# Retention attention and SwiGLU: y computed turned in 32-column TensorE tiles, scores over all rows, the own-token term on A's diagonal, the MLP one step earlier

## The chip, the cores and the metric

The kernel runs on one core of one Trainium2 chip. The metric is device time in microseconds (us). TensorE, VectorE, ScalarE and GpSimd appear in the profile as PE (PEld for its weight loads), DVE, ACT and POOL.

## The reference

Sizes are B=4, H=8, S=768, D=48 for the attention, and 3072 tokens, 384 model columns and 1536 hidden columns for the feed-forward block. Everything is fp32.

```python
for t in range(S):
    kt, vt, rt = k[:, :, t], v[:, :, t], r[:, :, t]
    cur = einsum('bhd,bhe->bhde', u * kt, vt)              # the token's own term
    y[:, :, t] = einsum('bhd,bhde->bhe', rt, state + cur)
    state = w * state + einsum('bhd,bhe->bhde', kt, vt)
x = y.transpose(0, 2, 1, 3).reshape(B * S, H * D)
g = x @ w_gate
out = (g * sigmoid(g) * (x @ w_val)) @ w_out
```

## The kernel before

The sequence is cut into 24 chunks of 128 tokens (6 in time x 4 batches), and the attention runs in chunked form. A head pair shares 128 partitions: 48 rows, 16 empty rows, 48 rows, 16 empty rows. The program is a pipeline of steps. In step s it prepares chunk s+1, turns chunk s, makes the scores of chunk s-1 and the outputs of chunk s-2, and turns x of chunk s-3. Between these parts it feeds *pieces* of the feed-forward block (MLP): a piece is six matmuls of `gv` or four of `o_ps`. Before the MLP can run, its 18 weight blocks are rounded by ACT, VectorE and GpSimd.

```python
def prepare(i):                       # GpSimd, then VectorE
    pool.tensor_mul(khat[i % 4][:], kl[:], kscale[:])
    pool.tensor_mul(rhat[i % 2][:], rl[:], rscale[:])
    pool.tensor_mul(rk[:], rl[:, :, 0:D], kl[:, :, 0:D])
    pool.tensor_mul(rk[:], rk[:], ub[:])
    dve.tensor_reduce(du[:], rk[:], axis=AX.X, op=ALU.add)
    ...
def scores(i, e):                     # e: which head of each pair
    q = slice(64 * e, 64 * e + D)     # 48 of the 128 rows
    for a in range(HP):
        pe.matmul(ps[:, a, :], kT[q, a, :], rT[q, a, :], start=True, stop=True, ...)
    dve.copy_predicated(At[i % 2][:, e], mask..., ps[:])
def own(i):                           # dv = du * v, on VectorE, two multiplies
    ...
def outputs(i):
    for a in range(HP):               # 128 tokens x 96 columns of y
        if c > 0:
            pe.matmul(ps[:, a, :], rT[:, a, :], Z[b][:, a, :], start=True, stop=False, ...)
        for e in range(2):
            pe.matmul(ps[:, a, :], A[:, e, a, :], vl[:, a, e, :], ...)
    dve.tensor_add(xs[i][:], ps..., dvs.pop(i)...)
def turn_x(i):                        # three transposes, then ACT
    for c in range(CC):
        pe.transpose(tp[:, c, :], x[:, P * c : P * (c + 1)], ident[:])
    act.copy(xT[:, i % NX, :, :], tp[:])
# ... the loop over steps (cut)
for s in range(N + 3):
    per = [0] * 6 if s < 4 else [1, 0, 1, 0, 1, 0] if s < 8 else [1] * 6 if s < 10 else [2] * 6
```

Of the kernel before, what the change touches and what calls it, by code (L numbers as in the profile page):

```python
# [9 lines left out]
FP32 = mybir.dt.float32  # L10
INT32 = mybir.dt.int32
# [4 lines left out]
P = 128  # L16
# [6 lines left out]
def fast(  # L23
# [24 lines left out]
    nc = tc.nc  # L48
    B, H, S, D = r.shape
    DP = 64  # L50
    HP = H // 2
    NCH = S // P
    N = B * NCH
    DM, DFF = moe_w_gate.shape
    CC, FC = DM // P, DFF // P

    cst = ctx.enter_context(tc.tile_pool(name="cst", bufs=1))
    two = ctx.enter_context(tc.tile_pool(name="two", bufs=2))
    three = ctx.enter_context(tc.tile_pool(name="three", bufs=3))
    ps_a = ctx.enter_context(tc.tile_pool(name="ps_a", bufs=5, space=bass.MemoryType.PSUM))  # L60
    ps_f = ctx.enter_context(tc.tile_pool(name="ps_f", bufs=2, space=bass.MemoryType.PSUM))
    ps_o = ctx.enter_context(tc.tile_pool(name="ps_o", bufs=1, space=bass.MemoryType.PSUM))
    dve, pool, act, pe, sp = nc.vector, nc.gpsimd, nc.scalar, nc.tensor, nc.sync


    wcol = cst.tile([P, HP], FP32, name="wcol")
    ub = cst.tile([P, H, D], FP32, name="ub")
    kscale = cst.tile([P, H, DP], FP32, name="kscale")
    rscale = cst.tile([P, H, DP], FP32, name="rscale")
    wL = cst.tile([P, HP, 2 * D], FP32, name="wL")  # L70
    sq = cst.tile([P, 8, HP], FP32, name="sq")
    bad = cst.tile([P, HP], FP32, name="bad")
    held = cst.tile([P, HP], FP32, name="held")
    badc = cst.tile([P, 1], FP32, name="badc")
    ones = cst.tile([P, 1], FP32, name="ones")
    ident = cst.tile([P, P], FP32, name="ident")
    mask = cst.tile([P, P], FP32, name="mask")
# [3 lines left out]
    NX = 12  # L81
    xT = cst.tile([P, NX, CC, P], FP32, name="xT")
    Z = [cst.tile([P, HP, 2 * D], FP32, name=f"Z{b}") for b in range(B)]
    r_ld = [cst.tile([P, H, DP], FP32, name=f"r_ld{i}") for i in range(2)]
    k_ld = [cst.tile([P, H, DP], FP32, name=f"k_ld{i}") for i in range(2)]

    v_ld = [cst.tile([P, HP, 2, 2 * D], FP32, name=f"v_ld{i}") for i in range(4)]
    khat = [cst.tile([P, H, DP], FP32, name=f"khat{i}") for i in range(4)]
    rhat = [cst.tile([P, H, DP], FP32, name=f"rhat{i}") for i in range(2)]
    At = [cst.tile([P, 2, HP, P], FP32, name=f"At{i}") for i in range(2)]  # L90

    def v_heads(i):
        t = v_ld[i % 4]
        return [t[:, :, e, D * e : D * (e + 1)] for e in range(2)]

    def load(i):
        c, b = divmod(i, B)
# [4 lines left out]
    def load_v(i):  # L102
        c, b = divmod(i, B)
        rows = slice(P * c, P * (c + 1))
        for e, dst in enumerate(v_heads(i)):
            sp.dma_start(
                out=dst, in_=v[b, :, rows, :].rearrange("(a e) t d -> e t a d", e=2)[e]
            )


# [51 lines left out]
    for t in k_ld + r_ld:  # L162
        dve.memset(t[:, :, D:DP], 0.0)
    for t in v_ld:
        dve.memset(t[:], 0.0)
    for e in range(2):
        sp.dma_start(out=wcol[64 * e : 64 * e + D, :], in_=w.rearrange("(a e) d -> e d a", e=2)[e])
    load(0)
# [1 line left out]
        out=ub[:].rearrange("p h d -> p (h d)"),  # L170
        in_=bass.AP(tensor=u.tensor, offset=u.offset, ap=[[0, P], [1, H * D]]),
# [14 lines left out]
    for l in range(7):  # L186
        n = 1 << l
        f = sq[:, l, :].unsqueeze(2).to_broadcast([P, HP, n])
# [8 lines left out]
    for e in range(2):  # L197
        q = slice(64 * e, 64 * e + 64)
# [6 lines left out]
        out=mask[:], in_=mask[:], compare_op=ALU.is_gt, fill=0.0,  # L205
        base=0, pattern=[[1, P]], channel_multiplier=-1,
    )
    for t in At:
        pool.memset(t[:], 0.0)


    dve.tensor_tensor(bad[:], held[:], wcol[:], ALU.not_equal)
# [4 lines left out]
    act.copy(outside, n_ps[0:1, 0, 0:1])  # L217


    dus, dvs, xs, turned = {}, {}, {}, {}  # L220

    def prepare(i):
        kl, rl = k_ld[i % 2], r_ld[i % 2]
# [9 lines left out]
        if i + 2 < N:  # L233
            load(i + 2)

    def turn(i):
        got = []
        for nm, t in (("kT", khat[i % 4]), ("rT", rhat[i % 2])):
            tp = ps_a.tile([P, HP, P], FP32, name="tp", tag="a")
            for a in range(HP):  # L240
                pe.transpose(  # L241
                    tp[:, a, :], t[:, 2 * a : 2 * a + 2, :].rearrange("p e d -> p (e d)"), ident[:]
                )
            x = (two if nm == "kT" else three).tile([P, HP, P], FP32, name=nm, tag=nm)
            act.copy(x[:], tp[:])
            got.append(x)
        turned[i] = got

    def scores(i, e):
        kT, rT = turned[i]  # L250
        q = slice(64 * e, 64 * e + D)
        ps = ps_a.tile([P, HP, P], FP32, name="s_ps", tag="a")
        for a in range(HP):
            pe.matmul(  # L254
                ps[:, a, :], kT[q, a, :], rT[q, a, :],
                start=True, stop=True, skip_group_check=True,
            )
        dve.copy_predicated(  # L258
            At[i % 2][:, e], mask[:].bitcast(INT32).unsqueeze(1).to_broadcast([P, HP, P]), ps[:]
        )  # L260

    def own(i):
        du = dus.pop(i)
        dvs[i] = two.tile([P, HP, 2, D], FP32, name="dv", tag="dv")
        for e, vh in enumerate(v_heads(i)):
            dve.tensor_mul(
                dvs[i][:, :, e, :], vh,
                du[:].rearrange("p (a e) -> p a e", e=2)[:, :, e : e + 1].to_broadcast([P, HP, D]),
            )

    def outputs(i):
        c, b = divmod(i, B)
        A, vl = At[i % 2], v_ld[i % 4]
        rT = turned.pop(i)[1]
        ps = ps_a.tile([P, HP, 2 * D], FP32, name="y_ps", tag="a")
        for a in range(HP):
            if c > 0:
                pe.matmul(  # L278
                    ps[:, a, :], rT[:, a, :], Z[b][:, a, :],
                    start=True, stop=False, skip_group_check=True,  # L280
                )
            for e in range(2):
                pe.matmul(  # L283
                    ps[:, a, :], A[:, e, a, :], vl[:, a, e, :],
                    start=(c == 0 and e == 0), stop=(e == 1), skip_group_check=True,
                )
        xs[i] = two.tile([P, DM], FP32, name="xs", tag="xs")
        dve.tensor_add(  # L288
            xs[i][:], ps[:].rearrange("p a x -> p (a x)"),
            dvs.pop(i)[:].rearrange("p a e d -> p (a e d)"),  # L290
        )

    def update(i):
        c, b = divmod(i, B)
        if c == NCH - 1:
            return
        kh, vl, z = khat[i % 4], v_ld[i % 4], Z[b]
        ps = ps_a.tile([P, HP, 2 * D], FP32, name="u_ps", tag="a")
        for a in range(HP):
            pe.matmul(  # L300
                ps[:, a, :].rearrange("p (e d) -> p e d", e=2),
                kh[:, 2 * a : 2 * a + 2, :].rearrange("p e d -> p (e d)"),
                bass.AP(
                    tensor=vl.tensor, offset=vl[:, a, 0, :].offset,
                    ap=[list(vl[:].ap[0]), [3 * D, 2], [1, D]],
                ),
                start=True, stop=True, skip_group_check=True,
            )
        if c == 0:
            dve.tensor_mul(z[:], ps[:], wL[:])  # L310
        else:
            dve.tensor_add(z[:], ps[:], z[:])  # L312
            pool.tensor_mul(z[:], z[:], wL[:])  # L313

    def turn_x(i):
        tp = ps_a.tile([P, CC, P], FP32, name="xtp", tag="a")
        x = xs.pop(i)
        for c in range(CC):
            pe.transpose(tp[:, c, :], x[:, P * c : P * (c + 1)], ident[:])  # L319
        act.copy(xT[:, i % NX, :, :], tp[:])  # L320


    hT = {}
# [41 lines left out]
    def feed(n):  # L365
        for _ in range(min(n, len(todo))):
            todo.popleft()()

    def queue(g):
        for f in range(FC):  # L370
            todo.append(lambda g=g, f=f: gate_value(g, f))
            if g > 0 and f >= 2 and f < 8:
                todo.append(lambda g=g, n=f - 2: project(g - 1, n // 3, n % 3))

    prepare(0)
    for s in range(N + 3):

        per = [0] * 6 if s < 4 else [1, 0, 1, 0, 1, 0] if s < 8 else [1] * 6 if s < 10 else [2] * 6
        if s + 1 < N:
            prepare(s + 1)  # L380
        if s < N:
            turn(s)
        round_weights(1 if s else 0)
        feed(per[0])
        if 1 <= s <= N:
            scores(s - 1, 0)
            feed(per[1])
            scores(s - 1, 1)
            own(s - 1)
            feed(per[2])  # L390
        if s >= 3:
            turn_x(s - 3)
            if s % 2 == 0:
                queue((s - 4) // 2)
            feed(per[3])
        if 2 <= s <= N + 1:
            outputs(s - 2)
            feed(per[4])
            update(s - 2)
        round_weights(1 if s > 1 else 0)  # L400
        feed(per[5])
    feed(len(todo))
    for j in range(2):
        for part in range(3):
# [414 lines left out]
```

## Time and profile before

The first line of the table is device time; the others are of one profiled execution.

| | before |
|---|---|
| time, median of 4 runs | 795.25 us (795.05 to 795.78) |
| span of the profiled run, mean granted clock | 793.2 us, 0.975 |
| turn of chunk 8, of chunk 10 | 122.7 us, 174.7 us |
| a full step after chunk 10 | 38.4 us |
| last matmul | 787.2 us |

"Turn of chunk i" is the first transpose of chunk i's keys on the TensorE timeline. I use it as a clock for the pipeline. From its first 175 us one should keep two things: the work is handed back and forth between GpSimd and VectorE, and TensorE has gaps.

### The profile page before, as it was taken

How to read it: one execution, taken by the hardware profiler on the slowest of the kernel's cores; microseconds unless marked ns; L12 is line 12 of the kernel's file. 1: busy time of each engine (PE TensorE's matmuls, PEld its weight loads, DVE VectorE, ACT ScalarE, POOL GpSimd, SP SyncE). 2: the span in 40 equal slices, each digit the busy share in tenths (PEclk: the TensorE clock that was granted, in tenths of full speed). 3: DMA queues.
4: the chain of work that ended last, by engine and by line, in shares of the span. 5: the costliest groups of instructions: out<-in, count | busy, mean ns of one | idle time of the engine just before them, and what ended most of it. 6: DMA issues, size and time to landing. Idle time of an engine off the chain costs nothing.

```text
span 793.2 us, 8984 instructions
## 1 busy us (share of the span) xinstructions
PE 749.0 (94%) x3666; PEld 604.1 (76%) x3666; DVE 250.3 (32%) x520; ACT 137.0 (17%) x281; POOL 159.0 (20%) x142
## 2 busy tenths in 40 slices
PE   3878888999999999999999999999999999999996
PEld 2777776877878878878878778778878878878773
DVE  5554565633222323222223223223223123212120
ACT  2432222411111111111111111111111111011010
POOL 5756454360202020202020202202202000000000
PEclk9958898999999999999999999999999999999999
DMA  8755454111101020102010102101000000000000
GB/s 206 149 154 134 119 151 113 50 41 31 30 11 41 1 40 11 31 11 41 0 41 11 31 10 41 31 11 41 10 11 22 1 11 10 1 11 11 10 11 23
DMA packets 85761, 33.89 MB, mean 43 GB/s; under 512 B 76368, under 2 KB 79568, under 8 KB 85712
## 3 DMA queue, kind: packets, MB, share of 16 engines
q1 hardware_dynamic: 82256, 28.52, 15.8%
q10 hardware_dynamic: 3456, 4.72, 1.7%
q8 instruction: 31, 0.51, 0.3%
q14 instruction: 18, 0.15, 0.1%
HBM read 28.51 MB, written 4.72 MB: 42 GB/s over the span
## 4 chain that ended last, share of the span: by engine, by line
PE 81%; DVE 8%; POOL 8%; issue 2%; ACT 1%; DMA 0%; SPq 0%; POOLq 0%; DVEq 0%
PE gv L333 45%; PE o_ps L352 22%; PE s_ps L254 4%; PE y_ps L283 4%; PE y_ps L278 2%; POOL khat L225 2%; POOL rhat L226 2%; PE tp L241 2%; DVE wo L156 1%; PE u_ps L300 1%; POOL rk L228 1%; POOL rk L227 1%; POOL wg L157 1%; PE xtp L319 1%; DVE wg L156 1%
## 5 line engine op out<-in xcount | busy, mean ns | idle before, releaser
L333 PE MATMUL gv<-xT,wg 128*128 128x256 f32 x864 | 217.6, 388 | 13.8 <-DVE hT L341 11.5
L333 PE MATMUL gv<-xT,wv 128*128 128x256 f32 x864 | 214.5, 385 | 0.0
L352 PE MATMUL o_ps<-wo,hT 128*128 128x384 f32 x576 | 197.1, 486 | 0.6 <-ACT o_sb L358 0.6
L333 PEld LDWEIGHTS gv<-xT,wg 128*128 128x128 f32 x864 | 158.1, 192 | 38.8 <-issue 11.5
L333 PEld LDWEIGHTS gv<-xT,wv 128*128 128x128 f32 x864 | 167.3, 194 | 23.8
L340 DVE TENSOR_TENSOR sg<-sg,gv 128x256 f32<-128x256 f32 x144 | 60.5, 420 | 326.6 <-ACT sg L339 326.6
L352 PEld LDWEIGHTS o_ps<-wo,hT 128*128 128x128 f32 x576 | 109.0, 190 | 62.9 <-ACT o_sb L358 1.2
L339 ACT ACTIVATE sg<-gv 128x256 f32<-128x256 f32 x144 | 55.2, 383 | 493.0 <-PE gv L333 480.7
L313 POOL TENSOR_TENSOR Z<-Z,wL 128x384 f32<-128x384 f32 x16 | 16.4, 1027 | 394.9 <-DVE Z L312 394.9
L283 PE MATMUL y_ps<-v_ld,At 128*128 128x96 f32 x384 | 61.7, 293 | 0.7 <-issue 0.7
L341 DVE TENSOR_TENSOR hT<-sg,gv 128x256 f32<-128x256 f32 x144 | 60.5, 420 | 4.9
L254 PEld LDWEIGHTS s_ps<-rT,kT 48*128 48x128 f32 x384 | 46.9, 210 | 18.1 <-issue 14.8
L254 PE MATMUL s_ps<-rT,kT 48*128 48x128 f32 x384 | 54.4, 310 | 2.2 <-DVE At L258 2.2
L283 PEld LDWEIGHTS y_ps<-v_ld,At 128*128 128x128 f32 x384 | 54.7, 209 | 1.0 <-issue 0.9
L258 DVE COPY_PREDICATED At<-mask,s_ps 128x512 f32<-128x512 int32 x48 | 33.5, 726 | 42.5 <-PE s_ps L254 42.3
L230 DVE TENSOR_REDUCE du<-rk 128x8 f32<-128x384 f32 x24 | 13.2, 552 | 83.1 <-POOL rk L228 83.1
L225 POOL TENSOR_TENSOR khat<-k_ld,kscale 128x512 f32<-128x512 f32 x24 | 30.5, 1272 | 6.2 <-ACT kscale L195 6.2
L226 POOL TENSOR_TENSOR rhat<-r_ld,rscale 128x512 f32<-128x512 f32 x24 | 30.5, 1272 | 2.1 <-ACT outside L217 2.1
L278 PE MATMUL y_ps<-Z,rT 128*128 128x96 f32 x160 | 30.4, 271 | 0.0
L278 PEld LDWEIGHTS y_ps<-Z,rT 128*128 128x128 f32 x160 | 25.7, 192 | 3.1
L288 DVE TENSOR_TENSOR xs<-y_ps,dv 128x384 f32<-128x384 f32 x24 | 13.3, 555 | 46.3 <-PE y_ps L283 46.3
L300 PEld LDWEIGHTS u_ps<-v_ld,khat 128*128 128x128 f32 x160 | 23.2, 211 | 2.7
(63 smaller groups left out, 356.5 us busy)
## 6 DMA issues: line engine op xcount, KB each, us to landing
k_ld<-in_k_dram SPq DMA_DIRECT2D x24, 192.0 KB, 3.2
r_ld<-in_r_dram SPq DMA_DIRECT2D x24, 192.0 KB, 3.6
w_bits<-in_moe_w_gate_dram SPq DMA_DIRECT2D x6, 768.0 KB, 5.0
w_bits<-in_moe_w_val_dram SPq DMA_DIRECT2D x6, 768.0 KB, 4.7
v_ld<-in_v_dram SPq DMA_DIRECT2D x48, 96.0 KB, 3.1
w_bits<-in_moe_w_out_dram SPq DMA_DIRECT2D x6, 768.0 KB, 4.5
out_dram<-o_sb ACTq DMA_DIRECT2D x24, 192.0 KB, 1.9
ub<-in_u_dram SPq DMA_DIRECT2D x1, 192.0 KB, 5.0
```

What stands on the lines that cost most here:

```text
L225: pool.tensor_mul(khat[i % 4][:], kl[:], kscale[:])
L226: pool.tensor_mul(rhat[i % 2][:], rl[:], rscale[:])
L254: pe.matmul(ps[:, a, :], kT[q, a, :], rT[q, a, :], start=True, stop=True, skip_group_check=True,)
L258: dve.copy_predicated(At[i % 2][:, e], mask[:].bitcast(INT32).unsqueeze(1).to_broadcast([P, HP, P]), ps[:])
L278: pe.matmul(ps[:, a, :], rT[:, a, :], Z[b][:, a, :], start=True, stop=False, skip_group_check=True,)
L283: pe.matmul(ps[:, a, :], A[:, e, a, :], vl[:, a, e, :], start=(c == 0 and e == 0), stop=(e == 1), skip_group_check=True,)
L300: pe.matmul(ps[:, a, :].rearrange("p (e d) -> p e d", e=2), kh[:, 2 * a : 2 * a + 2, :].rearrange("p e d -> p (e d)"), bass.AP(tensor=vl.t ...
L333: pe.matmul(gv[:, o, :].rearrange("p (i t) -> p i t", i=2), wt[:, c, P * f : P * (f + 1)], xT[:, 2 * g % NX : 2 * g % NX + 2, c, :], start ...
L339: act.activation(sg[:], gv[:, 0, :], AF.Sigmoid)
L340: dve.tensor_mul(sg[:], sg[:], gv[:, 0, :])
L341: dve.tensor_mul(hT[g][:, f, :], sg[:], gv[:, 1, :])
L352: pe.matmul(ps[:], hT[g][:, f, P * j : P * (j + 1)], wo[:, f, :], start=(f == 0), stop=(f == FC - 1),)
```

## The change

Its intent is to spend less TensorE time on attention. The scores use all 128 rows, with zeros where the other head of a pair sits. The own-token term is written on the diagonal of A by GpSimd, so no separate `dv` and no add are needed. And y is computed already turned: v and the state are the weights, in blocks of 32 columns, one block for each 32 of y_ps's 128 partitions (called column tiles below; `128*32` in the profile), so turning x falls away. The pipeline is one step shorter and the MLP is queued one step earlier.

```diff
+    def diagonal(i):
+        pool.tensor_mul(
+            At[i % 2][:], ident[:].unsqueeze(1).to_broadcast([P, H, P]),
+            dus.pop(i)[:].unsqueeze(2).to_broadcast([P, H, P]),
+        )
 def turn(i): ...
+            if nm == "kT":
+                for e in range(2):
+                    q = slice(64 * e, 64 * e + 64)
+                    act.copy(kT[i % 2][q, :, e, :], tp[q])
 def scores(i, half): ...
-                ps[:, a, :], kT[q, a, :], rT[q, a, :],
+                ps[:, n, :], kT[i % 2][:, a, e, :], turned[i][:, a, :],
 def outputs(i): ...
+        for cc in range(CC):
+            rows = []
+            for q in range(4):
+                a, s = divmod(4 * cc + q, 3)
+                each = [(z[:, a, 32 * s : 32 * s + 32], rT[:, a, :])] if c > 0 else []
+                if s < 2:
+                    each.append((vl[:, a, 32 * s : 32 * s + 32], A[:, 2 * a, :]))
+                if s > 0:
+                    each.append((vl[:, a, 32 * s + 16 : 32 * s + 48], A[:, 2 * a + 1, :]))
+                rows.append(each)
+            for n in range(3):
+                for q in range(4):
+                    if n < len(rows[q]):
+                        pe.matmul(ps[32 * q : 32 * q + 32, cc, :], *rows[q][n], ...)
+        act.copy(xT[:, i % NX, :, :], ps[:])
-    def own(i): ...      # and turn_x
 # ... (cut: v_ld's layout, clearing of kT instead of At and v_ld)
-        per = [0] * 6 if s < 4 else [1, 0, 1, 0, 1, 0] if s < 8 else [1] * 6 if s < 10 else [2] * 6
+        per = [0] * 5 if s < 3 else [1, 0, 1, 0, 1] if s < 8 else [1] * 5 if s < 10 else [3, 2, 2, 3, 2]
+        if 1 <= s <= N:
+            diagonal(s - 1)
         if s + 1 < N:
             prepare(s + 1)
-        if s >= 3:
-            turn_x(s - 3)
-            if s % 2 == 0:
-                queue((s - 4) // 2)
+        if s >= 2:
+            outputs(s - 2)
+            if s % 2:
+                queue((s - 3) // 2)
```

More of the change, by code (lines that the diff above doesn't have):

```diff
@@ L50, in fast @@
     DP = 64
+    VW = 2 * D + 16
     HP = H // 2
@@ L85, in fast @@
     k_ld = [cst.tile([P, H, DP], FP32, name=f"k_ld{i}") for i in range(2)]
-    v_ld = [cst.tile([P, HP, 2, 2 * D], FP32, name=f"v_ld{i}") for i in range(4)]
+    v_ld = [cst.tile([P, HP, VW], FP32, name=f"v_ld{i}") for i in range(4)]
     khat = [cst.tile([P, H, DP], FP32, name=f"khat{i}") for i in range(4)]
     rhat = [cst.tile([P, H, DP], FP32, name=f"rhat{i}") for i in range(2)]
-    At = [cst.tile([P, 2, HP, P], FP32, name=f"At{i}") for i in range(2)]
-    def v_heads(i):
-        t = v_ld[i % 4]
-        return [t[:, :, e, D * e : D * (e + 1)] for e in range(2)]
+    At = [cst.tile([P, H, P], FP32, name=f"At{i}") for i in range(2)]
+    kT = [cst.tile([P, HP, 2, P], FP32, name=f"kT{i}") for i in range(2)]
     def load(i):
@@ L104, in load_v @@
         rows = slice(P * c, P * (c + 1))
-        for e, dst in enumerate(v_heads(i)):
+        for e in range(2):
             sp.dma_start(
-                out=dst, in_=v[b, :, rows, :].rearrange("(a e) t d -> e t a d", e=2)[e]
+                out=v_ld[i % 4][:, :, 64 * e : 64 * e + D],
+                in_=v[b, :, rows, :].rearrange("(a e) t d -> e t a d", e=2)[e],
             )
@@ L164, in fast @@
     for t in v_ld:
-        dve.memset(t[:], 0.0)
+        dve.memset(t[:, :, D:64], 0.0)
     for e in range(2):
@@ L207, in fast @@
     )
-    for t in At:
-        pool.memset(t[:], 0.0)
+    for t in kT:
+        for e in range(2):
+            pool.memset(t[64 * e : 64 * e + 64, :, 1 - e, :], 0.0)
     dve.tensor_tensor(bad[:], held[:], wcol[:], ALU.not_equal)
@@ L217, in fast @@
     act.copy(outside, n_ps[0:1, 0, 0:1])
-    dus, dvs, xs, turned = {}, {}, {}, {}
+    dus, turned = {}, {}
     def prepare(i):
@@ L234, in prepare @@
             load(i + 2)
+    def diagonal(i):
[3 more added lines that the diff above has]
+        )
     def turn(i):
-        got = []
         for nm, t in (("kT", khat[i % 4]), ("rT", rhat[i % 2])):
@@ L243, in turn, with scores @@
                 )
-            x = (two if nm == "kT" else three).tile([P, HP, P], FP32, name=nm, tag=nm)
-            act.copy(x[:], tp[:])
-            got.append(x)
-        turned[i] = got
-    def scores(i, e):
-        kT, rT = turned[i]
-        q = slice(64 * e, 64 * e + D)
+            if nm == "kT":
+                for e in range(2):
+                    q = slice(64 * e, 64 * e + 64)
+                    act.copy(kT[i % 2][q, :, e, :], tp[q])
+            else:
+                turned[i] = three.tile([P, HP, P], FP32, name=nm, tag=nm)
+                act.copy(turned[i][:], tp[:])
+    def scores(i, half):
         ps = ps_a.tile([P, HP, P], FP32, name="s_ps", tag="a")
-        for a in range(HP):
+        for n in range(4):
+            a, e = divmod(4 * half + n, 2)
             pe.matmul(
-                ps[:, a, :], kT[q, a, :], rT[q, a, :],
+                ps[:, n, :], kT[i % 2][:, a, e, :], turned[i][:, a, :],
                 start=True, stop=True, skip_group_check=True,
@@ L258, in scores @@
         dve.copy_predicated(
-            At[i % 2][:, e], mask[:].bitcast(INT32).unsqueeze(1).to_broadcast([P, HP, P]), ps[:]
-        )
-    def own(i):
-        du = dus.pop(i)
-        dvs[i] = two.tile([P, HP, 2, D], FP32, name="dv", tag="dv")
-        for e, vh in enumerate(v_heads(i)):
-            dve.tensor_mul(
-                dvs[i][:, :, e, :], vh,
-                du[:].rearrange("p (a e) -> p a e", e=2)[:, :, e : e + 1].to_broadcast([P, HP, D]),
-            )
+            At[i % 2][:, 4 * half : 4 * half + 4],
@@ L271, in outputs @@
+            mask[:].bitcast(INT32).unsqueeze(1).to_broadcast([P, HP, P]), ps[:],
+        )
     def outputs(i):
         c, b = divmod(i, B)
-        A, vl = At[i % 2], v_ld[i % 4]
-        rT = turned.pop(i)[1]
-        ps = ps_a.tile([P, HP, 2 * D], FP32, name="y_ps", tag="a")
-        for a in range(HP):
-            if c > 0:
-                pe.matmul(
-                    ps[:, a, :], rT[:, a, :], Z[b][:, a, :],
-                    start=True, stop=False, skip_group_check=True,
-                )
-            for e in range(2):
-                pe.matmul(
-                    ps[:, a, :], A[:, e, a, :], vl[:, a, e, :],
-                    start=(c == 0 and e == 0), stop=(e == 1), skip_group_check=True,
-                )
@@ L287, in outputs @@
-        xs[i] = two.tile([P, DM], FP32, name="xs", tag="xs")
-        dve.tensor_add(
-            xs[i][:], ps[:].rearrange("p a x -> p (a x)"),
-            dvs.pop(i)[:].rearrange("p a e d -> p (a e d)"),
-        )
+        A, vl, z = At[i % 2], v_ld[i % 4], Z[b]
+        rT = turned.pop(i)
+        ps = ps_a.tile([P, CC, P], FP32, name="y_ps", tag="a")
+        for cc in range(CC):
[11 more added lines that the diff above has]
+                    if n < len(rows[q]):
+                        pe.matmul(
+                            ps[32 * q : 32 * q + 32, cc, :], *rows[q][n],
+                            start=(n == 0), stop=(n == len(rows[q]) - 1), skip_group_check=True,
+                        )
@@ L303, in update @@
                 bass.AP(
-                    tensor=vl.tensor, offset=vl[:, a, 0, :].offset,
-                    ap=[list(vl[:].ap[0]), [3 * D, 2], [1, D]],
+                    tensor=vl.tensor, offset=vl[:, a, 0:1].offset,
+                    ap=[list(vl[:].ap[0]), [64, 2], [1, D]],
                 ),
@@ L313, in update @@
             pool.tensor_mul(z[:], z[:], wL[:])
-    def turn_x(i):
-        tp = ps_a.tile([P, CC, P], FP32, name="xtp", tag="a")
-        x = xs.pop(i)
-        for c in range(CC):
-            pe.transpose(tp[:, c, :], x[:, P * c : P * (c + 1)], ident[:])
-        act.copy(xT[:, i % NX, :, :], tp[:])
     hT = {}
@@ L375, in fast @@
     prepare(0)
-    for s in range(N + 3):
-        per = [0] * 6 if s < 4 else [1, 0, 1, 0, 1, 0] if s < 8 else [1] * 6 if s < 10 else [2] * 6
+    for s in range(N + 2):
+        per = [0] * 5 if s < 3 else [1, 0, 1, 0, 1] if s < 8 else [1] * 5 if s < 10 else [3, 2, 2, 3, 2]
+        if 1 <= s <= N:
+            diagonal(s - 1)
         if s + 1 < N:
@@ L388, in fast @@
             scores(s - 1, 1)
-            own(s - 1)
             feed(per[2])
-        if s >= 3:
-            turn_x(s - 3)
-            if s % 2 == 0:
-                queue((s - 4) // 2)
+        if s >= 2:
+            outputs(s - 2)
+            if s % 2:
+                queue((s - 3) // 2)
             feed(per[3])
-        if 2 <= s <= N + 1:
-            outputs(s - 2)
-            feed(per[4])
             update(s - 2)
         round_weights(1 if s > 1 else 0)
-        feed(per[5])
+        feed(per[4])
     feed(len(todo))
```

## The prediction

> **What bounds the kernel now.** I read the engine table and the 40 slices first, then two windows of busy time, then single stretches of the TensorE timeline, then the chain that ended last.
>
> ```profile
> PE 749.0 (94%) x3666; PEld 604.1 (76%) x3666; DVE 250.3 (32%) x520; ACT 137.0 (17%) x281; POOL 159.0 (20%) x142
> PE   3878888999999999999999999999999999999996
> ...
> 0.00:175.00 175.00, 139.22 (x730) 118.53 (x731) 93.89 (x167) 54.80 (x87) 90.46 (x79) 0.89 0.51 127
> 175.00:790.00 615.00, 609.83 (x2938) 485.57 (x2936) 156.45 (x353) 82.22 (x194) 68.58 (x64) 1.00 0.08 19
> ```
>
> The window columns are length, then busy us of PE, PEld, DVE, ACT and POOL, then the granted clock. After 175 us TensorE never rests (609.8 of 615 us), so there each microsecond of TensorE issue time is one of the span. Before it TensorE is waiting or running below full clock. The kernel has two regimes, and I price the change in each.
>
> A busy PE is not an issue rate, so I take distances between starts on the timeline (start, us, engine, line, operation):
>
> ```profile
> 410.42 0.81 PE L352 MATMUL o_ps<-wo,hT 128*128 128x384 f32 x2
> 411.16 1.16 PE L254 MATMUL s_ps<-rT,kT 48*128 48x128 f32 x8
> 412.25 1.13 PE L333 MATMUL gv<-xT,wg 128*128 128x256 f32 x4
> ...
> 429.49 0.36 PE L278 MATMUL y_ps<-Z,rT 128*128 128x96 f32 x2
> ...
> 432.14 1.49 PE L333 MATMUL gv<-xT,wg 128*128 128x256 f32 x6
> 433.47 1.46 PE L333 MATMUL gv<-xT,wv 128*128 128x256 f32 x6
> 434.76 1.46 PE L333 MATMUL gv<-xT,wg 128*128 128x256 f32 x6
> ...
> 669.20 1.71 PE L254 MATMUL s_ps<-rT,kT 48*128 48x128 f32 x16
> 670.84 0.55 PE L319 MATMUL xtp<-ident,xs 128*128 128x128 f32 x3
> ```
>
> Each fp32 matmul is two passes (864 records for 432 matmuls of wg). Twelve passes of 256 columns take 434.76 - 432.14 = 2.6 us, so 0.216 us a pass; a piece of MLP work (six matmuls of gv, or four of o_ps at 0.322 us a pass) is 2.6 us. The 24 passes of y take 432.14 - 429.49 = 2.65 us, 0.110 each although only 96 columns stream (0.08 us at the gv rate)[...]. A transpose is one pass of 0.109.
>
> Scores show a second cost. The two o_ps passes from 410.42 end their issue at 411.07, the eight s_ps passes would need 0.90 us, but gv starts at 412.25, and in the single records its second pass follows 0.32 us later instead of 0.216. So the visit costs 1.29 us, 0.39 more than its passes. It happens only around s_ps, the one group that uses 48 of the 128 rows.
>
> Turns of chunks 10, 11 and 12 begin at 174.7, 213.1 and 251.5: a full step is 38.4 us, with twelve pieces (31.1 us). The other 7.3 us are attention, and the parts add up: turns 0.87, scores 2 x 1.29, y 2.65, state update 0.87, turning x 3 x 0.109 = 0.33, together 7.3. Nothing in the step is idle time.
>
> In the start the chain alternates between GpSimd and VectorE:
>
> ```profile
> 59.01 1.23 POOL khat L225
> 60.24 1.22 POOL rhat L226
> 61.46 0.97 POOL rk L227
> 62.50 1.00 POOL rk L228
> 63.53 0.55 DVE du L230
> 64.08 0.87 DVE wv L155
> 65.05 0.96 DVE wv L156
> 66.01 1.27 DVE At L258 x2
> 67.28 1.17 DVE dv L266 x2
> 68.45 0.47 DVE xs L288
> ```
>
> Each waits while the other works: VectorE begins a step with du, which needs GpSimd's prepare, and GpSimd's next add needs VectorE's rounding. One turn of this ring is 14 to 19 us.
>
> [...]where both halves of scores follow each other, 16 passes take 1.64 us (669.20 to 670.84), less than their 1.79 us in sequence plus any switch. In the single records the second half's first pass starts three passes before the first half has issued its last, so TensorE went out of program order there.[...]
>
> **The change part by part.** A full step after chunk 4, TensorE:
>
> Scores over all rows keep 16 passes of 128 columns: 16 x 0.110 = 1.76 us instead of 2.58. The row tile is gone and with it two visits' penalty: -0.8 us.
>
> Turning x goes: y leaves TensorE already turned. -0.33 us.
>
> y becomes 28 matmuls of 32 weight columns and 128 moving columns (12 blocks of 32 outputs; those straddling two heads take three matmuls, others two). That is 56 passes instead of 24, in four column tiles. Each tile gets exactly 7 matmuls, 14 passes. Four abreast: 14 x 0.110 = 1.54 us, and with the first load and the ragged ends I take 1.9 us: -0.75 us. Two abreast it is 28 x 0.110 = 3.1 us, one at a time 6.2 us.
>
> [...]I take the measured 0.39 us.
>
> Sum per full step: -0.8 - 0.33 - 0.75 + 0.39 = -1.5 us, 38.4 to 36.9.
>
> Off TensorE, in a step that TensorE fills: VectorE loses dv (2 x 0.42) and xs (0.555); ACT copies kT in two halves (+0.58) and xT straight out of y_ps (as long as before); GpSimd gains the diagonal, 128x1024. Its rows give 1.272 us for 512 and 1.000 for 384 elements, so 0.00213 us an element and 2.4 us for 1024 (estimate). GpSimd is busy 5.5 of 38 us, so all of this is beside other work.
>
> From 174.7 us to the last matmul at 787.2 the kernel before still has 194 pieces, 16 y, 17 turns of x, 15 scores, 14 turns and 12 updates: about 612 us by the costs above, just what the trace has. So the saving is countable: y 16 x 0.75 = 12.0; turning x 17 x 0.33 = 5.6; scores 15 x 0.8 = 12; switches -16 x 0.39 = -6.2; and, since MLP work starts one step earlier (the pipeline is 26 steps instead of 27), one piece more is done by step 10 (23 instead of 22): 2.6. Together 26 us.
>
> The start: the ring gains 2.4 us of diagonal a step, on GpSimd ahead of prepare, and loses 1.17 + 0.47 of dv and xs: +0.7 us a step, about +6 us over eight steps. Against it, VectorE's clearing of v_ld (2.8 us) shrinks, of which perhaps 0.7 us was ahead of the first scale; and the third piece of a step now stands after the second rounding, so its two multiplies (0.84 us) can run while GpSimd works: up to 4 us over five steps. TensorE's savings there mostly turn into waiting. Net +1 us, uncertain by 7 either way.
>
> 795.4 - 26 + 1 = 770 us.
>
> **The rivals.** *Column tiles in program order.* If a matmul cannot pass an earlier one, the two passes of one fp32 matmul hold up the next tile, and only the second pass of one overlaps the first of the next: y 3.1 us, 19 us of the gain gone, about 789 us, within 2%. [...]against it the early start in the two adjacent score halves. About one in four. *No overlap, or an issue limit:* 112 loads and matmuls in place of 48 might be bound by the rate of issue. At 6.2 us y the kernel loses 43 us more: about 840. The 5 ns between neighbouring starts in the adjacent halves speaks against it. One in twenty. *The start eats it:* with the diagonal the GpSimd-VectorE ring becomes the bound for longer, steps 3 to 8 lengthen by 2 us each, and TensorE saturates some 12 us later: 782. The ring's lines speak for it; the earlier MLP start and TensorE being nearly full from 125 us speak against. *A new wait in the step:* y goes straight to xT, so where the queue is empty the next gv waits for ACT's copy of 0.48 us; three odd late steps do that, at about 1 us, but the xT copy already does it before (2.3 us of gv's idle time in all).
>
> **Range and chances.** Full overlap with a tidy start gives 760 to 772, partial overlap 772 to 785, program order 785 to 795. The 2% line is 779.5 us, which y at 2.5 us and a start of +1 reaches. Range 759 to 790; faster 0.72, within 2% 0.23, slower 0.05.
>
> **What would show it.** Right: the full step near 36.9 us; y from first start to the next group near 1.9 us plus about 0.4; no gap around s_ps; no xtp; 17% or more fewer microseconds of attention in the step. Neighbouring y starts a few ns apart, four to each 0.11 us, would prove four tiles abreast; pairs would prove the first rival. The turn of chunk 10 should stay within 7 us of 174.7. Wrong: y over 2.6 us, gaps on TensorE behind y or behind the diagonal, or a granted clock under 1.00 after 175 us.

The sum came to 795.4 - 26 + 1 = 770 us. That the load of 128 weight columns sets the 0.110 us of a pass was not shown; the records show only that passes of 96 and of 128 moving columns take the same 0.110 us. That four column tiles run abreast (y in 1.9 us, of which 1.9 - 1.54 = 0.36 is an allowance for the ends) was the estimate from the overlap of the 48-row scores, 16 passes in 1.64 us: the second half's first pass starts at 669.749 us, with three passes of the first half, from 669.855 on, still to start. And the +0.39 us a chunk for y in column tiles is an estimate too, the extra cost of a visit of the 48-row scores taken over. Where the texts speak of a switch, they mean this cost; what TensorE does in that time no run shows.

## The result and the profile after

The changed kernel takes 755.0 us (753.81 to 755.3, 4 runs) against 795.25 us in the same rounds. The ratio is 0.949 (95% interval 0.9474 to 0.9507). A ratio is the mean time of one kernel's fast runs over that of the other's of the same rounds, so not quite the ratio of the medians quoted. The direction and the main mechanism were predicted. The size was not: 755 us is below the range of 759 to 790.

The engine table, the slices of TensorE, and the two windows that answer to those of before (columns as in the prediction):

```profile
PE 704.4 (94%) x4298; PEld 563.0 (75%) x4298; DVE 218.1 (29%) x448; ACT 153.9 (20%) x305; POOL 203.6 (27%) x168
PE   2775978999999999999999999999999999999997
...
0.00:175.00 175.00, 135.14 (x959) 110.94 (x960) 81.16 (x147) 65.33 (x104) 112.56 (x94) 0.92 0.51 130
175.00:749.00 574.00, 569.29 (x3340) 452.06 (x3338) 136.89 (x301) 88.56 (x201) 91.00 (x74) 1.00 0.08 20
```

TensorE is as full as before after 175 us, with 632 more matmul records and less time in them. GpSimd is busier by 45 us, which is the diagonal. Next, the TensorE timeline of one visit to y and one to the scores (start, us, engine, line, operation):

```profile
402.79 1.46 PE L332 MATMUL gv<-xT,wv 128*128 128x256 f32 x6
404.18 0.43 PE L293 MATMUL y_ps<-rT,Z 128*32 128x128 f32 x8
404.42 0.40 PE L293 MATMUL y_ps<-At,v_ld 128*32 128x128 f32 x8
...
405.51 0.43 PE L293 MATMUL y_ps<-At,v_ld 128*32 128x128 f32 x8
405.87 1.56 PE L332 MATMUL gv<-xT,wg 128*128 128x256 f32 x6
...
425.85 2.74 PE L351 MATMUL o_ps<-wo,hT 128*128 128x384 f32 x8
428.43 1.05 PE L263 MATMUL s_ps<-rT,kT 128*128 128x128 f32 x8
429.32 1.46 PE L332 MATMUL gv<-xT,wg 128*128 128x256 f32 x6
```

Eight passes of y start in each 0.24 us, although one pass of 128 columns takes 0.110 us. In the single records the first four start at 404.181, 404.187, 404.194 and 404.201, the next four from 404.314: four tiles run abreast. All 56 passes take 405.87 - 404.18 = 1.69 us. The visit also costs at both ends: the gv passes before would end their issue at 402.79 + 6 x 0.216 = 404.09, so y begins 0.09 us late, and the second gv pass after y comes 0.32 instead of 0.216 us after the first, 0.10 more. The whole visit costs 1.69 + 0.09 + 0.10 = 1.88 us. Around the scores nothing is left of a gap: o_ps needs 8 x 0.322 = 2.58 us and s_ps starts 2.58 us after it; s_ps takes 0.89 us, its eight passes.

The chain that ended last, in a step near the start, shows the diagonal where the prediction put it, ahead of prepare and in front of VectorE's du:

```profile
46.07 1.90 POOL At L239
47.97 1.22 POOL khat L226
...
51.45 1.00 POOL rk L229
...
52.48 0.55 DVE du L231
```

The diagonal stands six times in this chain before the turn of chunk 8, 6 x 1.90 = 11.4 us.

Where the 40 us went follows from the turns of chunks and the last matmul:

| | before | after | difference |
|---|---|---|---|
| start to turn of chunk 8 | 122.7 (10 pieces done) | 127.7 (13 pieces done) | +5.0 |
| steps 8 and 9 | 52.0 (12 pieces) | 36.7 (10 pieces) | -15.3 |
| turn of chunk 10 to last matmul | 612.5 | 582.3 | -30.2 |
| full step | 38.4 | 36.5 | -1.9 |

So the steady part gave 30 us where I had counted 26, and the start gave 10 us where I had counted a loss of 1. The experiments take these two apart.

### The profile page after: what moved, and what is told of

Read it like the earlier page. It is cut to its first block, busy times and chain, and to the rows that moved or that the text cites. A ratio compares the mean times of both kernels' runs of the same rounds, so it can differ in the third digit from the quotient of the medians.

```text
span 752.1 us, 10222 instructions
## 1 busy us (share of the span) xinstructions
PE 704.4 (94%) x4298; PEld 563.0 (75%) x4298; DVE 218.1 (29%) x448; ACT 153.9 (20%) x305; POOL 203.6 (27%) x168
## 4 chain that ended last, share of the span: by engine, by line
PE 85%; POOL 6%; DVE 5%; issue 2%; ACT 1%; DMA 0%; SPq 0%; DVEq 0%; POOLq 0%
PE gv L332 48%; PE o_ps L351 25%; PE y_ps L293 4%; PE s_ps L263 4%; PE tp L248 2%; PE u_ps L306 2%; POOL At L239 2%; POOL rhat L227 1%; POOL khat L226 1%; POOL rk L229 1%; POOL rk L228 1%; DVE wv L156 1%; DVE wg L156 1%; DVE wv L155 1%; DVE wg L155 1%
## 5 line engine op out<-in xcount | busy, mean ns | idle before, releaser
L332 PEld LDWEIGHTS gv<-xT,wg 128*128 128x128 f32 x864 | 161.5, 193 | 50.4 <-issue 20.0
L319 POOL TENSOR_TENSOR Z<-Z,wL 128x384 f32<-128x384 f32 x16 | 16.5, 1032 | 342.2 <-DVE Z L318 342.2
L239 POOL TENSOR_TENSOR At<-ident,du 128x1024 f32<-128x1024 f32 x24 | 45.5, 1898 | 37.6 <-PE y_ps L293 37.6
L263 PEld LDWEIGHTS s_ps<-rT,kT 128*128 128x128 f32 x384 | 50.4, 197 | 7.0 <-DVE At L267 0.7
L263 PE MATMUL s_ps<-rT,kT 128*128 128x128 f32 x384 | 51.0, 281 | 0.3 <-DVE At L267 0.3
L293 PE MATMUL y_ps<-At,v_ld 128*32 128x128 f32 x768 | 36.7, 283 | 5.2 <-issue 2.8
L293 PEld LDWEIGHTS y_ps<-At,v_ld 128*32 128x32 f32 x768 | 30.4, 113 | 6.5 <-issue 3.6
L254 ACT COPY kT<-tp 64x512 f32<-64x512 f32 x48 | 27.9, 580 | 12.6 <-PE tp L248 11.3
L293 PE MATMUL y_ps<-rT,Z 128*32 128x128 f32 x480 | 30.1, 279 | 0.0
L293 PEld LDWEIGHTS y_ps<-rT,Z 128*32 128x32 f32 x480 | 19.3, 109 | 8.3 <-issue 7.8
```

The source lines that it names most:

```text
L239: pool.tensor_mul(At[i % 2][:], ident[:].unsqueeze(1).to_broadcast([P, H, P]), dus.pop(i)[:].unsqueeze(2).to_broadcast([P, H, P]),)
L254: act.copy(kT[i % 2][q, :, e, :], tp[q])
L263: pe.matmul(ps[:, n, :], kT[i % 2][:, a, e, :], turned[i][:, a, :], start=True, stop=True, skip_group_check=True,)
L293: pe.matmul(ps[32 * q : 32 * q + 32, cc, :], *rows[q][n], start=(n == 0), stop=(n == len(rows[q]) - 1), skip_group_check=True,)
L332: pe.matmul(gv[:, o, :].rearrange("p (i t) -> p i t", i=2), wt[:, c, P * f : P * (f + 1)], xT[:, 2 * g % NX : 2 * g % NX + 2, c, :], start ...
```

## The experiments

The theory of the result was this. In the steady part each saved microsecond of TensorE counts, with four column tiles abreast. In the start the diagonal lengthens the GpSimd-VectorE ring, but the MLP, begun one step earlier, fills TensorE's idle time, which is worth far more than the single piece I had counted. The rivals: the ring does not matter and TensorE's own work decides the start; or the start gained only because attention got shorter. All outputs are right.

### b_pad: the scores alone

```diff
+    kTp = [cst.tile([P, HP, 2, P], FP32, name=f"kTp{i}") for i in range(2)]
-                ps[:, a, :], kT[q, a, :], rT[q, a, :],
+                ps[:, a, :], kT[:, a, e, :], rT[:, a, :],
```

Not shown: kT is copied in two halves, and the ring of turned x has 10 chunks instead of 12.

> The kernel before with only the scores changed to all 128 rows (the ring of turned x cut from 12 to 10 chunks to make room). Theory: a visit of the 48-row scores costs 0.39 us beyond its passes, so about 0.8 us a step in the 13 steps where the two halves stand apart and about 0.2 us in the 11 where they stand together: 13 x 0.8 + 11 x 0.2 = 12 us faster, about 783 us. Rival ([...]the added ACT copy and the smaller ring cost as much): 793 to 797 us.

Measured: 787.83 us (ratio 0.9913), 7 us faster rather than 12. The full step fell from 38.4 to 37.6 us, the 0.8 us expected. The steps with adjacent halves did not change at all (28.1 and 22.9 us in both), so the 0.2 us there was wrong. From chunk 10 on the gain is 8.6 us (612.5 to 603.9), which is 11 steps with separate halves x 0.78. The turn of chunk 10 came 1.2 us later than before. The 0.39 us a visit are right. In the start of the kernel *before* shorter scores, with the extra copy and the smaller ring, buy nothing.

### a_rows: the change with the scores back on 48 rows

```diff
-            a, e = divmod(4 * half + n, 2)
+            a, e = n, half
+            q = slice(64 * e, 64 * e + D)
-                ps[:, n, :], kT[i % 2][:, a, e, :], turned[i][:, a, :],
+                ps[:, n, :], kT[i % 2][q, a, e, :], turned[i][q, a, :],
```

> The changed kernel with the scores on 48 rows again, one head parity for each half. Theory (two switches of 0.39 us in each step where the halves stand apart, 15 steps here): 15 x 0.78 = 12 us more, full step 37.3 us, 765 to 769 us. Rival (as in the kernel before, where padding alone gave 7 us): 760 to 763 us.

Measured: 765.83 us (0.9643), 10.8 us more than the change, full step 37.3 us. Of this 9.8 us come after the turn of chunk 10 (592.1 against 582.3 us). The padding is worth about 11 us inside the change. It is worth more there than in the kernel before: the halves stand apart in more of the late steps (9.8 against 8.6 us), and the start no longer loses 1.2 us but gains 1.7, most of it in steps 8 and 9 (19.15 against 18.37 us each), which TensorE fills.

### a_tilewise and a_pairs: how y's four tiles come to overlap

```diff
 a_tilewise                                        a_pairs
+        for q in range(4):                        +        for h in range(2):
+            for cc in range(CC):                  +            for cc in range(CC):
+                for n, pair in ...(work[cc, q]):  +                for n in range(3):
+                    pe.matmul(...)                +                    for q in (2 * h, 2 * h + 1):
+                                                  +                        pe.matmul(...)
```

> The changed kernel with the matmuls of y ordered tile after tile (14 passes of one column tile, then the next), the same 56 passes. Theory (TensorE looks only about three passes ahead, as the adjacent score halves show): hardly any overlap, y about (56 - 9) x 0.11 = 5.2 us instead of 1.7, 3.5 us more a chunk, 815 to 835 us. [...]Rival 2 (overlap does not depend on the order at all): 755 us.

> The changed kernel with y ordered for two column tiles at a time, tiles 0 and 1 for all of y, then 2 and 3; the same 56 passes. Theory (four tiles run abreast in the changed kernel, within reach of three passes): two abreast, y about 2 x 14 x 0.11 = 3.0 us instead of 1.7, 1.35 us more a chunk, 780 to 787 us, full step 37.8 us. Rival (something else than the number of tiles paces y): 755 to 760 us.

Measured: tile after tile 812.12 us (1.0221, interval 1.02 to 1.0243), slower than the kernel before and 3 us under the range expected; two tiles at a time 772.1 us (0.9718). The first and next starts on the timeline of a_tilewise, then of a_pairs:

```profile
429.31 0.41 PE L296 MATMUL y_ps<-rT,Z 128*32 128x128 f32 x2
...
434.33 1.56 PE L335 MATMUL gv<-xT,wg 128*128 128x256 f32 x6
```

```profile
336.30 0.41 PE L298 MATMUL y_ps<-rT,Z 128*32 128x128 f32 x4
...
339.08 1.56 PE L338 MATMUL gv<-xT,wg 128*128 128x256 f32 x6
```

The same 56 passes take 5.02 us tile after tile, 2.78 us two abreast and 1.69 us in the change's order. The 5.2 us expected for a reach of about three passes was close; with rival 2, that the order does not matter, it would have stayed at 1.69. The single records, told apart by their order, show the reach itself: the second tile's first pass starts at 430.437, while three passes of the first tile (430.540, 430.650, 430.759) had still to start; it is three at the other two edges too. The two-abreast kernel missed its expected time (780 to 787) on the good side: y was 2.78 instead of 3.0 us, the full step 37.6 instead of 37.8, and in the start the longer y cost less than 1 us (turn of chunk 10 at 165.1). The order of the matmuls is what makes the tiles pay; without it the change would have lost.

### a_diag2 and a_diaglate: the diagonal in the ring

```diff
 a_diag2
+        for _ in range(2):
             pool.tensor_mul(At[i % 2][:], ident..., du...)
 a_diaglate
-        if 1 <= s <= N:
-            diagonal(s - 1)
         if s + 1 < N:
             prepare(s + 1)
+        if 1 <= s <= N:
+            diagonal(s - 1)
```

> The changed kernel with the diagonal computed twice, 1.9 us of GpSimd more a step. Theory ring: until about step 7 GpSimd and VectorE in turn set the step, so the turn of chunk 8 comes 7 x 1.9 = 13 us later and most of it stays: 764 to 768 us. Rival (TensorE's own work decides already there): the time stays within 754 to 758 us. Both: full steps after chunk 10 stay at 36.5 us.

> The changed kernel with the diagonal behind prepare in GpSimd's order instead of ahead of it. VectorE's du then doesn't wait for it, and the copy of the scores comes 2.4 us later anyway. Theory ring (doubling the diagonal cost 16.5 us, nearly all before chunk 10): 1.9 us a step come off in steps 1 to 7, 740 to 748 us, all of it before the turn of chunk 10. Rival (the diagonal only moves to another wait, of the score copy or of the add of the weights): 752 to 757 us.

Measured: the doubled diagonal 771.54 us (0.9711), 16.5 us more; the diagonal behind prepare 743.55 us (0.9364), 11.4 us less than the change. In the first the turn of chunk 8 moved from 127.7 to 141.9 us; in the second to 117.2. The doubled diagonal cost more than the 9 to 13 us expected (764 to 768). The two profiled runs are 17.7 us apart; 15.3 of it lie before the turn of chunk 10, and the rest are three full steps of 37.3 us, which neither theory had foreseen. The chain of a_diaglate has no diagonal in it any more (links under 0.1 us left out):

```profile
53.68 1.80 POOL wg L157
55.48 1.22 POOL khat L226
...
58.96 1.02 POOL rk L229
...
60.00 0.55 DVE du L231
```

The ring sets the start up to the turn of chunk 8, and the diagonal in it costs the change about 11 us, as much as the six diagonals in its chain. The rival that TensorE's own work decides is out.

### a_late: the change with the late start of the MLP

```diff
-        per = [0] * 5 if s < 3 else [1, 0, 1, 0, 1] if s < 8 else [1] * 5 if s < 10 else [3, 2, 2, 3, 2]
+        per = [0] * 5 if s < 4 else [1, 0, 1, 0, 1] if s < 8 else [2, 1, 1, 1, 1] if s < 10 else [3, 2, 2, 3, 2]
-            if s % 2:
-                queue((s - 3) // 2)
+            if s % 2 == 0 and s >= 4:
+                queue((s - 4) // 2)
# ... (cut: the last queue in step N + 1)
```

> The changed kernel with its MLP work queued and fed as before: first piece in step 4, ten pieces by step 8, six in steps 8 and 9 each. Theory (the earlier start of the MLP is what kept the start from losing time): three pieces of 2.6 us less are done by the turn of chunk 8, 760 to 765 us. Rival (the start's gain is only TensorE's shorter attention work): 754 to 757 us.

Measured: 766.26 us (0.9639), 11.3 us more than the change and a little over the 760 to 765 expected. The turn of chunk 10 came at 176.7 us instead of 164.4. After it both kernels took 582.3 us, by coincidence: a_late has one piece more to do there, and none of the four waits for xT. Where the 12.3 us arise is worth a look. Without the three early pieces chunk 8 turns at 119.5 us instead of 127.7, so up to there the early pieces, with the weight blocks that they ask for, delay the pipeline by 8.1 us, no less than their 3 x 2.6. The gain is in steps 8 and 9: 36.7 us with 10 pieces against 57.2 us with 12. The two windows around steps 8 and 9, first of the change, then of a_late:

```profile
125.00:150.00 25.00, 25.00 (x175) 20.60 (x174) 14.03 (x23) 10.68 (x18) 17.18 (x12) 0.97 0.29 75
150.00:175.00 25.00, 25.00 (x167) 19.19 (x166) 6.84 (x14) 4.43 (x10) 12.27 (x11) 1.00 0.26 53
```

```profile
125.00:150.00 25.00, 18.94 (x140) 15.66 (x139) 10.63 (x20) 6.13 (x10) 8.43 (x8) 0.86 0.25 62
150.00:175.00 25.00, 20.79 (x133) 15.92 (x132) 12.32 (x15) 6.37 (x12) 13.30 (x9) 0.86 0.20 49
```

In the change TensorE is full from 125 us on. In a_late it idles 10 of the 50 us, and the granted clock is at 0.86 besides. This is one such place on a_late's timeline:

```profile
132.71 2.90 PE L332 MATMUL gv<-xT,wg 128*128 128x256 f32 x6 [6.06 <-DVE hT L340]
```

TensorE waited 6.06 us for VectorE to empty a gv buffer, while VectorE waited 7.54 us for GpSimd's diagonal and prepare (its du starts at 129.70). The six passes after the gap took 2.90 us by the record; six gv passes at 124.30 us, before it, took 1.46. That the gap made them slow was not shown.

The chain of a_late shows a second effect of the late start. Its first `o_ps` piece finds four weight blocks not yet rounded, and VectorE takes them one after another:

```profile
146.92 0.48 DVE wo L155
...
147.49 1.57 DVE wo L156
...
155.56 2.40 DVE wo L156
...
159.86 1.90 POOL At L239
```

GpSimd's diagonal and prepare stand behind this burst. The kernel before has the same burst (149.6 to 160.6 us). In the change the pieces asked for blocks earlier, and the last burst is two blocks (141.3 to 145.8 us), with TensorE full beside it. How the 12 us divide between pieces done earlier and blocks rounded earlier was not tested.

With the late start, the change's turn of chunk 10 is 2.0 us later than before (174.7). That is near the +1 us that I had predicted for the start as a whole. The early start of the MLP, with the earlier rounding that it brings, is therefore the missing term.

### b_early and b_early_act: the early MLP in the kernel before

```diff
 b_early
-        if s >= 3:
-            turn_x(s - 3)
-            if s % 2 == 0:
-                queue((s - 4) // 2)
         ...
             update(s - 2)
+            turn_x(s - 2)
+            if s % 2:
+                queue((s - 3) // 2)
 b_early_act, on top of it
-        dve.tensor_add(xs[i][:], ps..., dvs.pop(i)...)
+        act.copy(xs[i][:], ps[:].rearrange("p a x -> p (a x)"))
+    # du on A's diagonal, by GpSimd ahead of prepare; own() removed
```

> The kernel before with turn_x moved into the step of its outputs, and the MLP queued and fed as in the changed kernel, so 13 pieces instead of 10 by the turn of chunk 8; nothing else. Theory (the earlier start of the MLP is worth some 11 us, as taking it from the changed kernel showed): 781 to 787 us, nothing in the full steps of 38.4 us. Rival (it only pays together with the shorter attention work): 792 to 796 us.

> The kernel before with turn_x in the same step and the early MLP, and now du on the diagonal of A (made by GpSimd ahead of prepare, as in the change), so that ACT instead of VectorE takes y out of PSUM and dv and its add are gone. y is not turned and the scores are not padded. Theory (moving turn_x alone gained only 6 us because turning x waits for VectorE's add, 14.6 us of gaps before chunk 8): with ACT the gaps close and the start gains what it lost, 778 to 784 us, although the ring has 0.7 us more a step. Rival (the ring alone sets the start): 790 to 796 us.

Measured: 789.28 us (0.9936) and 787.53 us (0.9902). The early start alone gave 6 us, less than the 8 to 14 expected and more than the rival's. Its single TensorE records show why it was not more: turning x waits for VectorE's add, with waits of 6.2, 7.6, 2.2 and 4.3 us before chunk 8. With ACT taking y out of PSUM these waits are gone, but others, of 3.4 and 4.1 us for VectorE's hT, stand between the turned x and the next gv, and only 1.7 us were gained, against 5 to 11 expected. So the early start is worth 11 us in the change, and in the kernel before 6 us alone, 8 us together with the diagonal and ACT's copy. What makes up the rest I did not separate; the shorter attention work of the change is a candidate, not a finding.

### a_best and a_best_merged: a faster version

Both have the diagonal behind prepare. `a_best` also puts the scores back on 48 rows, in one visit that alternates between the two blocks of 48 rows (row tiles), each with its own PSUM tile. `a_best_merged` is its control, with all rows in one visit.

```diff
+        for a in range(HP):
+            for e in range(2):
+                q = slice(64 * e, 64 * e + D)
+                pe.matmul(ps[e][:, a, :], kT[i % 2][q, a, e, :], turned[i][q, a, :], ...)
-            feed(per[1])
-            feed(per[2])
+            feed(per[1] + per[2])
```

> The changed kernel with the diagonal behind prepare and with the scores back on 48 rows, but both head parities in one visit, their matmuls alternating between the two row tiles and two PSUM banks. Theory (tiles run abreast here too, one pair of switches of 0.39 us): 8 x 0.112 + 0.39 = 1.3 us a step instead of 1.79, full step 36.0 us, 733 to 738 us. Rival (row tiles don't overlap beyond the edge seen before): one visit of 1.79 + 0.39 us, 750 to 754 us.

> The same with the scores kept on all 128 rows, both halves in one visit: the control for the order of the work. Theory (all-row scores have no visit cost): within 1.5 us of the kernel with the diagonal behind prepare, 742 to 745 us. Rival (where the visit stands matters by itself): a difference of over 3 us.

Measured: 734.54 us (0.9236) and 742.2 us (0.9338). The timeline of a_best:

```profile
410.87 2.74 PE L353 MATMUL o_ps<-wo,hT 128*128 128x384 f32 x8
413.54 1.16 PE L264 MATMUL s_ps<-rT,kT 48*128 48x128 f32 x16
414.63 1.56 PE L334 MATMUL gv<-xT,wg 128*128 128x256 f32 x6
```

Sixteen passes of scores take 1.09 us, where eight of the kernel before took the same 1.09 (411.16 to 412.25 in the prediction's lines). With the late start behind o_ps (0.09) and the slower first gv pass (0.10) the visit is 1.28 us; 1.3 was expected, and the full step is 36.0 us, also as expected. The control lies 1.4 us under a_diaglate (743.55), so the order of the work is worth little, and 7.7 us come from the row tiles. This version beats the change by 20 us and the kernel before by 60.

## Why the prediction was right or wrong

**TensorE bounds the kernel after 175 us: right.** The part from the turn of chunk 10 to the last matmul fell by 30.2 us through TensorE's shorter attention and one piece less.

**Scores, "-0.8 us" a step: right in size, wrong in count.** b_pad and a_rows both moved the full step by 0.8 us. The sum of 15 x 0.8 = 12 us was too large: the kernel before pays the 0.39 us a visit only in the 11 late steps where its halves stand apart, 8.6 us by b_pad.

**Turning x, "-0.33 us": taken as counted.** No run isolates it; the records of xtp are gone.

**y, "I take 1.9 us" plus "the measured 0.39 us": mis-sized.** The visit measured 1.88 us in all, not 2.29. The 1.9 already held 0.36 us for the first load and the ragged ends, so the cost at the ends was counted twice. Beyond its passes (14 x 0.110 = 1.54) the visit costs 0.34 us in all, ragged ends included, near the 0.39 of the scores. A load of 32 weight columns lasts 0.110 us by the record (median of the change's y) and one of 128 columns 0.192 (median of y before). Counted once, this is 0.4 us x 16 chunks = 6.4 us more gain. With 3.4 us less from the scores, 26 becomes 29; the last 1 us of the 30.2 I cannot assign.

**Four tiles abreast, out of program order: right.** It was the assumption with the most at stake. The four starts within 0.02 us, a_tilewise (y 5.02 us, its second tile started ahead of three passes of the first) and a_pairs (2.78 us) decide for it, and against the rival of column tiles in program order (predicted y 3.1 us) and the one of an issue limit (6.2 us). The 43 us of that rival are the loss against the kernel before; against the 770 it would have been 16 x 4.3 = 69.

**The start, "Net +1 us": the step that failed.** Its own sign failed with it: the turn of chunk 10 should have stayed within 7 us of 174.7, and came at 164.4. The sum of its ring terms fits: with the MLP started late, that turn moved by +2.0 us. This is partly luck, for the diagonal alone cost 11.4 us, not 8 x 2.4 = 19, and so the loss of dv and xs and the rest gave about 9 us (11.4 - 2.0; no run isolates it), not the 18 counted. What failed is "one piece more is done by step 10 (23 instead of 22): 2.6". I priced the early start by counting pieces at chunk 10 and called the rest waiting. But it puts three pieces before chunk 8, leaves two fewer to steps 8 and 9 and has the weights rounded sooner, and in these two steps TensorE no longer runs dry. Taking it away cost 12.3 us at the turn of chunk 10 (176.7 instead of 164.4) and 11.3 us in the whole. So the sentence "TensorE's savings there mostly turn into waiting" held only for the late start. In the sum: -26 becomes -30, and +1 becomes -10, which is the measured -40. The 4 us of the steady part alone would have left 766 us.

**The rival "the start eats it": wrong in sign, right in mechanism.** The diagonal is in the ring, and doubling it cost 16.5 us. Its estimated 2.4 us were 1.90.

**A new wait behind y: as expected, and no change.** Where the queue is empty gv waits four times for ACT's copy of y, 2.4 us in all, where it waited four times for the copy of the turned x before, 2.3 us in all.

## What to carry to other kernels

When small matmuls go into tiles, interleave them so that the next tile's work stands within three passes, the reach seen at each edge of a_tilewise; the same matmuls tile after tile took three times as long here (5.02 against 1.69 us). Price the start of a pipeline by when the bounding engine first runs without gaps, not by the number of items done at a milestone: here an earlier start of three pieces, worth 2.6 us each as work, was worth 11 us. And look at what stands first in an engine's queue: moving the diagonal behind prepare was worth 11 us without changing any work.
